# Batch 0 of a fused attention and two-MoE kernel in plain fp32 matmuls, with w_in decoded in another way and a new order of the steps up to batch 1

## The chip, the cores and the metric

The kernel runs on one core of a Trainium2 chip. The metric is the device time of one execution in microseconds, the median of several runs. A core has TensorE (PE; its weight loads are the rows PEld), VectorE (DVE), ScalarE (ACT), GpSimd (POOL) and SyncE (SP), whose queue here issues nearly all DMAs. Each engine takes its instructions in the order in which they were written.

## What is computed

Eight batches of 576 tokens pass an attention with 32 memory slots for each of 8 heads of 64, then a MoE layer with a squared relu (512 to 2048 to 512), then a second one with a softmax-weighted activation and a layer norm (512 to 1024 to 512). The weights are float64.

```python
a = softmax(phi)                    # [8, 8, 576, 32], over axis 2 (the tokens)
k_m = einsum('bhsm,bhsd->bhmd', a, k);  v_m = einsum('bhsm,bhsd->bhmd', a, v)
attn = softmax(q @ k_m.T / 8) @ v_m              # per head: 576 x 32 times 32 x 64
x = attn.transpose(0, 2, 1, 3).reshape(4608, 512)
h = x @ w_in                                     # 4608 x 2048
g = s * relu(h) ** 2 + b
x = g @ w_out                                    # 4608 x 512
# second MoE: h = x @ w_in2; solu = h * softmax(h); (layer norm of solu * g_ln) @ w_out2
```

## The kernel before

For a batch the attention's output is never formed. V·w_in is multiplied first (`vw_mm`, L613: a block matrix of v_m against 512 columns of w_in, four products j = 0 to 3), and the probabilities, transposed, are then multiplied by it: `gemm1_mm` (L982) makes hp, 128 features by 288 tokens, for each half j of the batch and each of 8 pairs of feature blocks. Relu and square (`relu` L993, `square` L1018 or L1020, `square_hi` L1010) make g; `gemm2_mm` (L1043) sums g against w_out into y, for each half j and each of four blocks d of 128 outputs; y goes to DRAM for the second MoE, which follows after batch 7.

fp32 accuracy is had from fp16 matmuls: each operand is split into a high and a low half after a scaling by a power of two (`split_hi` on ScalarE L310, `split_lo` on VectorE L313), and a product is three passes, high by high, high by low and low by high. One hp of two blocks is 12 matmuls of 288 columns, one y 48. The scale needs a bound: for w_in the maximum over all of it, for w_out one over each half. The float64 weights are decoded on the chip from pairs of 32-bit words, in pieces of 128 x 1024: for w_in an absolute value (`decode_abs`, ScalarE, L245), a max pass that also clamps (`decode_max`, VectorE, L255), a shift and a merge of the sign (`decode_bits`, L271 and L262), and the three low bits, either by an OR (`piece_or`, VectorE, L1139) or by a shift and an add on GpSimd (L250 or L252, L268). For w_out it is a scaled copy (`decode_rebias`, ScalarE), a shift and a merge (`decode_shift`, L283, L284) and the OR.

The order up to batch 1 is written out by hand: `FIRST` is a list of steps of which each is one function (`STEPS`), and all engines take their instructions in the order of the list. `Lw.cx` loads piece (c, x) of w_in, `Ai`, `Bi`, `Ci`, `Pi` or `PiX` decode it, `Lo`, `Ao` ... the same for w_out, `km` multiplies k and v by phi, `qm` transposes q, `s0` to `s6` and `sT` are scores and softmax of a third of a batch, `vm` is V·w_in, `g` an hp, `ya` and `yb` the halves of a y, `yo` its eviction, `xh` and `xl` the fp16 halves of w_out, `oad`, `oap`, `oa` the maximum over partitions by a ones-matmul. The digits behind the point are batch or half, then index. `KEEP` gives some steps filler matmuls in front. From batch 1 on a loop runs the same functions, and w_in's and w_out's split halves stay in SBUF. While batch 0 is in work, batch 1's attention is prepared too.

```python
PASSES = ((0, 0), (0, 1), (1, 0))
for step in FIRST.split():
    name, _, at = step.partition(".")
    now[0] = step
    STEPS[name](*(int(a) for a in at))
```

Of the kernel before, what the change touches and what calls it, by code (L numbers as in the profile page):

```python
# [37 lines left out]
s4.01 s1.00 s5P.01 sT.01 phe.1 s0.02 Pi.01 km.10 s1.02 vm.00 s2.00 Lkv.12 ks.10 s3.00 s6P.00 s4.00 s5P.00 im PiX.11
vs0 iad vh.00 s2.02 Pi.30 vm.01 Lkv.13 ko.10 iap vl.00 ia vm.02 km.11 sT.00 vh.01 iv vs.0 Lo.10 ks.11 vl.01 vh.02
vl.02 Ci.31 Lo.01 g.02 Ao.11 Co.11 gr.02 ko.11 PiX.31 gq.02 PoX.11 Ao.10 g.00 gh.02 Lo.00 gr.00 Co.10 Bo.11 gqP.00  # L40
s3.02 g.01 g.05 vm.03 Ao.01 ghD.00 glP.00 gr.01 Co.01 gl.02 g.03 vh.03 gr.05 s6P.02 Lo.21 gqP.01 s4.02 Ao.00 gh.05
PoX.10 mb.1 s5P.02 gqP.05 gh.01 vl.03 Lkv.22 glP.05 Lo.20 gr.03 g.07 Co.00 PoX.01 vb.1 glP.01 gr.07 gqP.03 Bo.00
# [12 lines left out]
yd.10 sT.12 Lq.21
# [10 lines left out]
def tile_mem_attention__moe_relu2__solu_ln(  # L66
# [56 lines left out]
    relu01 = const.tile([128, 1], FP32)  # L123
# [12 lines left out]
    first = gp.tile([128, 1152], FP32, tag="aT", name="first", bufs=2)  # L136
    ones_f = first[:, 256:384]
# [11 lines left out]

    kv_s = kv_p.tile([128, 3, 2, 2, C * D], FP32, name="kv_s")  # L150
# [211 lines left out]
    def load_q(n, i):  # L362
# [1279 lines left out]
```

## Time and profile before

| | |
|---|---|
| median of 3 runs | 1136.35 us (1135.41 to 1138.27) |
| span of the profiled execution | 1132.3 us |
| median less that span | 4.05 us |
| TensorE busy, share of the span | 1074.8 us, 95% |
| VectorE | 793.9 us, 70% |
| ScalarE | 518.6 us, 46% |
| GpSimd | 237.9 us, 21% |
| first matmul of batch 1 | at 189.74 us |

The profile is of one execution. Its rows name a line of the kernel, the engine, the tile written and the tiles read, with sizes and times; an entry in square brackets at a row's end is the time for which the engine had stood idle and the instruction that it waited for. An fp32 matmul has two records. A matmul's record holds its latency too, so a run of records is shorter than the sum of their means. "PEclk" is the granted clock of TensorE: 1.00 is 2.4 GHz, 0.50 is 1.2 GHz. A share of busy time over the whole span mixes stages with different limits, so stretches are read apart.

### The profile page before, as it was taken

To read this page: it belongs to the slowest core of one execution; us is meant where nothing else is said; L and a number is where in the kernel's file an instruction comes from. 1 tells how busy PE (TensorE), PEld (TensorE's weight loads), DVE (VectorE), ACT (ScalarE), POOL (GpSimd) and SP (SyncE) were. 2 spreads that over 40 slices of the span, in tenths; PEclk is the share of its full clock that TensorE was granted. 3 is DMA by queue.
4 is the path that set the end of the run, shared out by engine and by line. 5 is a ranking of instruction groups with operands and counts; after the bars stand their busy time and mean duration, and the time that the engine had idled before them with its cause. 6 is when DMAs were issued, how large, how long until landed. Compare 5 with 4: busy or idle time off the path is not lost.

```text
span 1132.3 us, 20705 instructions
## 1 busy us (share of the span) xinstructions
PE 1074.8 (95%) x8334; PEld 704.9 (62%) x8334; DVE 793.9 (70%) x1516; ACT 518.6 (46%) x753; POOL 237.9 (21%) x182
## 2 busy tenths in 40 slices
PE   4885799998999999999999999999999999999998
PEld 3743567776777777777777777764444444444443
DVE  6899867776876777777677675647666666666662
ACT  2447546455465356365355555623333333333332
POOL 2337341003012012011012020003222222222221
PEclk9688899999999999999999999999999999999999
DMA  9975045594372572643753314114444444445335
GB/s 293 258 204 155 4 107 128 129 216 111 100 178 69 132 156 59 165 124 92 152 143 96 83 25 173 55 52 99 105 100 94 109 106 98 98 112 103 74 76 103
DMA packets 219488, 134.01 MB, mean 118 GB/s; under 512 B 144896, under 2 KB 207616, under 8 KB 219392
## 3 DMA queue, kind: packets, MB, share of 16 engines
q1 hardware_dynamic: 219184, 132.48, 48.0%
q8 instruction: 65, 1.06, 0.4%
q14 instruction: 31, 0.25, 0.1%
q10 hardware_dynamic: 112, 0.20, 0.0%
q0 software_dynamic: 96, 0.01, 0.0%
HBM read 71.83 MB, written 23.07 MB: 84 GB/s over the span
## 4 chain that ended last, share of the span: by engine, by line
PE 75%; DVE 11%; DMA 6%; ACT 3%; issue 2%; SPq 1%; POOL 1%; ACTq 0%; POOLq 0%; DVEq 0%
PE y L1043 26%; PE y L1461 16%; PE hp L1379 16%; PE hp L982 10%; DMA kv_s<-in_k_dram 1%; PE wp L672 1%; DVE g L1025 1%; PE kp L475 1%; DMA work<-in_moe_w_out_dram 1%; PE sp L818 1%; DMA w_in_t<-wt_s 1%; DMA w_out<-in_q_dram 1%; DMA q_s<-in_q_dram 1%; DVE wt_s L313 1%; PE sp L862 1%
## 5 line engine op out<-in xcount | busy, mean ns | idle before, releaser
L1043 PE MATMUL y<-g,w_out 128*128 128x288 f16 (+1 forms) x2880 | 365.5, 287 | 7.5 <-DVE first L197 7.5
L1043 PEld LDWEIGHTS <-w_out 128*128 128x128 f16 x3072 | 297.9, 98 | 101.2 <-issue 21.3
L982 PE MATMUL hp<-aT,vwt 128*128 128x288 f16 x1536 | 197.9, 290 | 19.0 <-ACT r L993 12.6
L1379 PE MATMUL hp<-w_t,xs 128*128 128x512 f16 x864 | 192.0, 379 | 0.0
L1461 PE MATMUL y<-w_t,lt 128*128 128x512 f16 x864 | 191.7, 379 | 0.0
L982 PEld LDWEIGHTS <-vwt 128*128 128x128 f16 x1536 | 152.1, 99 | 62.0 <-issue 15.4
L1461 PEld LDWEIGHTS <-lt 128*128 128x128 f16 x864 | 84.6, 98 | 101.7
L1379 PEld LDWEIGHTS <-xs 128*128 128x128 f16 x864 | 84.5, 98 | 101.4
L1423 POOL TENSOR_TENSOR rstd<-ve,nhalf 128x1 f32<-128x1 f32 x36 | 52.6, 1462 | 333.4 <-DVE mv L1421 333.4
L1393 DVE TENSOR_REDUCE hmx<-hp 128x1 f32<-128x1024 f32 x36 | 44.1, 1224 | 83.9 <-PE hp L1379 83.9
L310 ACT ACTIVATE xs<-xt,xsc 128x512 f16<-128x512 f32 x36 | 25.9, 720 | 150.8 <-PE hp L1379 129.3
L1018 ACT ACTIVATE r<-r 128x576 f32<-128x576 f32 x118 | 80.6, 683 | 21.5 <-DVE g L1025 15.2
L1025 DVE TENSOR_TENSOR g<-r,g 128x576 f16<-128x576 f32 x113 | 87.4, 773 | 3.8
L1060 ACT ACTIVATE x<-y,bcol,cs 128x288 f32<-128x288 f32 x64 | 37.5, 585 | 114.7 <-PE y L1043 102.1
L993 ACT ACTIVATE r<-hp 128x576 f32<-128x576 f32 x120 | 77.1, 642 | 13.6 <-PE hp L982 8.1
L307 DVE TENSOR_REDUCE xmx<-x 128x1 f32<-128x288 f32 x64 | 28.8, 450 | 58.1 <-ACT x L1060 57.2
L967 DVE CAST g<-r 128x576 f16<-128x576 f32 x112 | 51.5, 460 | 20.7 <-ACT r L1018 20.7
L895 POOL TENSOR_TENSOR e<-e,ssm 96x512 f32<-96x512 f32 x22 | 24.8, 1128 | 195.5 <-DVE ssm L890 195.5
L1400 ACT ACTIVATE e<-hp,nm,xiv 128x1024 f32<-128x1024 f32 x36 | 43.3, 1203 | 46.1 <-DVE nm L1395 46.1
L1469 ACT ACTIVATE o<-y,io 128x512 f32<-128x512 f32 x36 | 24.7, 687 | 53.0 <-issue 40.5
L1437 DVE TENSOR_TENSOR nat<-so,nat 128x1024 f16<-128x1024 f32 x36 | 43.7, 1215 | 5.4 <-ACT nat L1432 5.4
L1416 DVE BATCH_NORM_STATS2 bs<-so 128x6 f32<-128x512 f32 x72 | 46.3, 685 | 1.2
(246 smaller groups left out, 1215.6 us busy)
## 6 DMA issues: line engine op xcount, KB each, us to landing
x_d<-x SPq DMA_DIRECT2D x64, 144.0 KB, 2.1
xt<-x_d SPq DMA_DIRECT2D x36, 256.0 KB, 3.2
kv_s<-in_k_dram SPq DMA_DIRECT2D x31, 288.0 KB, 5.9
kv_s<-in_v_dram SPq DMA_DIRECT2D x31, 288.0 KB, 6.5
q_s<-in_q_dram SPq DMA_DIRECT2D x42, 144.0 KB, 3.3
phi_sb<-in_phi_dram SPq DMA_DIRECT2D x8, 576.0 KB, 5.8
out_dram<-o SPq DMA_DIRECT2D x23, 192.0 KB, 2.9
raw<-in_moe_w_out_dram SPq DMA_DIRECT2D x4, 1024.0 KB, 6.8
```

What stands on the lines that cost most here:

```text
L967: nc.vector.tensor_copy(out=g_of(n, j, 0)[:, 2 * fp:2 * fp + 2, 0:BLK], in_=gt["r2", j, fp])
L982: nc.tensor.matmul(out=hp[:, u, 0:BLK], lhsT=vt[:, pw, R, f * 128:(f + 1) * 128], rhs=aT[:, CJ * j:CJ * (j + 1), pa, R, :], start=(x == 0) ...
L993: nc.scalar.activation(out=r, in_=gt.pop(("h", j, fp))[:, :, 0:BLK], func=ACTF.Relu, scale=scale)
L1018: nc.scalar.activation(out=r2, in_=r, func=ACTF.Square)
L1025: (nc.vector if eng == "D" else nc.gpsimd).tensor_tensor(out=g_of(n, j, 1)[:, fs, 0:BLK], in0=gt.pop(("r2", j, fp)), in1=g_of(n, j, 0)[:, ...
L1043: nc.tensor.matmul(out=y[:, 0:w], lhsT=w_out_t[d][:, pw, f, :], rhs=g_of(n, j, pg)[:, f, 0:w], start=(x == 0), stop=(x == len(steps) - 1),)
L1379: nc.tensor.matmul(out=hp[:, a, :], lhsT=xs[:, px, kk, :], rhs=wt[:, pw, kk, a * 512:(a + 1) * 512], start=(kk == 0 and px == 0 and pw == ...
L1393: nc.vector.tensor_reduce(out=mx, in_=hv, op=ALU.max, axis=AX)
L1416: nc.vector.bn_stats(out=bs[:, a, :], in_=so[:, a * 512:(a + 1) * 512])
L1423: nc.gpsimd.tensor_tensor(out=rstd, in0=ve, in1=nhalf, op=ALU.pow)
L1437: nc.vector.tensor_tensor(out=nat[:, 1, :], in0=so, in1=nat[:, 0, :], op=ALU.subtract)
L1461: nc.tensor.matmul(out=y[:, 0:DM], lhsT=lt[:, pl, f, :], rhs=wt[:, pw, f, :], start=(x == 0), stop=(x == len(steps) - 1),)
```

## The change

Batch 0 no longer splits anything. Its hp is an fp32 product of fp32 V·w_in (`first_vw`, a copy out of PSUM) and fp32 transposed probabilities (`first_tr` transposes them on TensorE, `first_aT` copies them); g is fp32 (`first_sq`), and y multiplies it by the decoded fp32 w_out (`first_y`). The fp16 halves of w_out, which later batches use, are still made. The scale of batch 0's V·w_in and relu goes, and the bias column and the factor of y's eviction with it become simpler. w_in is decoded as w_out was: scaled copy, shift and merge, OR on VectorE; its maximum is a plain reduction of the decoded piece at any later time, and GpSimd decodes nothing. The steps s4, s5, sT of batch 0 and its gq, gh, gl go. q of batch 0 is loaded in longer rows, and its transposes are plain matmuls by the identity in two column halves. Some buffers move: w_out's fourth decoded piece lies in a fixed square buffer `r2_s`, k, v and q of batches 0 and 1 lie elsewhere. `KEEP` has 37 filler matmuls where it had 130. `FIRST` is a new list.

```diff
 KEEP = {
-    "km.00": 78, "km.00+": 8, "km.01": 18, "mm.0": 8, "s0.01": 6, "oap.0": 6, "oap.1": 6,
+    "pht.0": 7, "pho.0": 3, "km.01": 1, "mm.0": 11, "qm.00": 4, "qm.02": 6, "at.1": 5,
 }
...
-Lw.21 Lphi.0 Lq.00 Lw.00 LiD.21 Lw.20 Lw.30 Ai.21 qm.00 Bi.21 Ai.20 Lw.01 Ai.30 Ai.00 Lw.10 Ci.21 Ai.10 phm.0 pht.0
+Lphi.0 phm.0 Lw.00 pht.0 Ai.00 Lq.00 Lw.10 Lq.01 phd.0 Lkv.01 pho.0 phb.0 Lkv.00 Ai.10 Lkv.02 phe.0 qm.01 qo.01 qm.00
...
+    def first_tr(cp):
+        ev = sc_e[0, cp].rearrange("p (c h) m -> p c (h m)", c=2)
+        tp = ps_h.tile([128, 2, 512], FP32, tag="h", name="ta")
+        keep(tp[:, 1])
+        for c in range(2):
+            for R in range(2):
+                nc.tensor.transpose(
+                    out=tp[:, 0, (2 * R + c) * P:(2 * R + c + 1) * P], in_=ev[:, c, R * 128:(R + 1) * 128],
+                    identity=ident[0:P, 0:P],
+                )
+        sc_e[0, cp] = tp
...
+    def first_vw(j, R, copy):
...
+        copy(out=vw_t[0][:, R, j * 512:(j + 1) * 512], in_=wp_t[0, j][:, R, :])
...
+    def first_h(j, fp):
+        hp = ps_h.tile([128, 2, 512], FP32, tag="h", name="hp")
...
+            for R in range(2):
+                nc.tensor.matmul(
+                    out=hp[:, u, 0:BLK],
+                    lhsT=vw_t[0][:, R, f * 128:(f + 1) * 128],
+                    rhs=aT0[:, R, CJ * j:CJ * (j + 1), :].rearrange("p c t -> p (c t)"),
+                    start=(R == 0),
+                    stop=(R == 1),
+                )
...
+    def first_sq(j, fp):
+        x = 2 * (fp % 4)
+        nc.scalar.activation(out=g32_of(j, fp // 4)[:, x:x + 2, 0:BLK], in_=gt.pop(("r", j, fp)), func=ACTF.Square)
...
+    def first_y(j, d, part):
...
+        w = BLK + 1 - j
+        wt = wt_t[d, part].rearrange("p (k d) -> p k d", k=8)
+        for f in range(8):
+            nc.tensor.matmul(
+                out=y[:, 0:w], lhsT=wt[:, f, :], rhs=g32_of(j, part)[:, f, 0:w],
+                start=(part == 0 and f == 0), stop=(part == 1 and f == 7),
+            )
...
     def piece_max(c, x):
...
-        decode_max(piece("i", c, x)[0], pk_t["i"][:, 2 * c + x:2 * c + x + 1])
+        src = piece("i", c, x)[0]
+        nc.vector.tensor_reduce(
+            out=pk_t["i"][:, 2 * c + x:2 * c + x + 1], in_=src, op=ALU.max, axis=mybir.AxisListType.XY,
+            apply_absolute_value=True,
+        )
...
-        (decode_abs if w == "i" else decode_rebias)(*piece(w, c, x))
+        decode_rebias(*piece(w, c, x))
...
-        (decode_bits if w == "i" else decode_shift)(*piece(w, c, x))
+        decode_shift(*piece(w, c, x))
```

VectorE's queue at its start, before: a piece of w_in with its max pass (L255), then phi's tree of maxima (L393 to L395).

```order
L252 TENSOR_SCALAR raw<-raw 128x1024
L255 TENSOR_SCALAR w_in_t,pk<-w_in_t 128x2x512
L271 TENSOR_SCALAR w_in_t<-w_in_t 128x2x512
L262 SCALAR_TENSOR_TENSOR w_in_t<-raw,w_in_t 128x2x512
L393 TENSOR_TENSOR t<-phi_sb 96x512
L394 TENSOR_TENSOR t<-t,phi_sb 96x512
L395 TENSOR_TENSOR pm<-t 96x256
L412 TENSOR_REDUCE first<-tx 128x2
L416 TENSOR_TENSOR first<-ident,first 128x256
L444 TENSOR_TENSOR phi_sb<-phi_sb,tx 96x1536
```

The same place now (L383 to L435 is phi, L280, L281 and L1189 a piece of w_in):

```order
L383 TENSOR_TENSOR t<-phi_sb 96x512
L384 TENSOR_TENSOR t<-t,phi_sb 96x512
L385 TENSOR_TENSOR pm<-t 96x256
L402 TENSOR_REDUCE first<-tx 128x2
L406 TENSOR_TENSOR first<-ident,first 128x256
L435 TENSOR_TENSOR phi_sb<-phi_sb,tx 96x1536
L280 TENSOR_SCALAR w_in_t<-w_in_t 128x2x512
L281 SCALAR_TENSOR_TENSOR w_in_t<-raw_g,w_in_t 128x2x512
L1189 SCALAR_TENSOR_TENSOR w_in_t<-raw_g,w_in_t 128x2x512
L280 TENSOR_SCALAR w_in_t<-w_in_t 128x2x512
```

Phi went ahead of all of w_in, and no max pass stands between a piece's shift and the copy before it.

TensorE where batch 0's first y begins, before: the last rows of an hp and the first of y, each matmul with its weight load, w_out in fp16.

```order
L982 LDWEIGHTS vwt
L982 MATMUL hp<-aT,vwt 128x288
L1043 LDWEIGHTS w_out_118
L1043 MATMUL y<-g,w_out_118 128x289
L1043 LDWEIGHTS w_out_118
L1043 MATMUL y<-g,w_out_118 128x289
```

The same place now, from batch 0's last V·w_in (wp) on; hp is L935, k and v by phi L464, y L967, mp (L189) a maximum over partitions:

```order
L603 MATMUL wp<-w_in_t,first 64x512 x4
L935 MATMUL hp<-aT_116,vw_478 128x288 x4
L464 MATMUL kp<-kv_s,phi_sb 32x128 x24
L489 MATMUL kp<-ones,phi_sb 32x1 x24
L935 MATMUL hp<-aT_116,vw_478 128x288 x12
L189 MATMUL mp<-first 128x128
L935 MATMUL hp<-aT_116,vw_478 128x288 x12
L967 MATMUL y<-g_545,wt_s 128x289 x8
L967 MATMUL y<-g_785,wt_s 128x289 x8
L189 MATMUL mp<-first 128x128
L935 MATMUL hp<-aT_116,vw_478 128x288 x4
```

y now reads the decoded w_out (wt_s) in fp32, eight matmuls for a half of the features instead of 24, and the maximum for w_out's scale (the second mp) stands behind the first y instead of ahead of it.

## Rows read from the trace of the kernel before

**Rows 1.** Busy us by stretch (PE, PEld, DVE, ACT, POOL), granted clock, DMA share, GB/s.

```profile
40.00:60.00 20.00, 17.97 (x130) 15.46 (x130) 17.33 (x35) 7.83 (x12) 5.60 (x4) 0.50 0.80 214
70.10:189.70 119.60, 93.88 (x686) 66.20 (x687) 97.18 (x143) 68.54 (x99) 52.24 (x32) 0.90 0.40 105
80.00:100.00 20.00, 11.10 (x59) 7.20 (x59) 17.90 (x22) 12.60 (x20) 14.76 (x9) 0.74 0.84 228
...
120.00:140.00 20.00, 12.54 (x92) 9.38 (x90) 16.52 (x24) 8.34 (x13) 8.03 (x5) 0.83 0.01 1
...
189.70:275.70 86.00, 81.62 (x790) 62.77 (x789) 63.97 (x118) 46.89 (x66) 10.46 (x10) 1.00 0.70 166
275.70:362.00 86.30, 84.89 (x820) 65.45 (x819) 61.99 (x123) 46.06 (x71) 15.09 (x11) 1.00 0.47 120
```

**Rows 2.** TensorE in order of time: start us, us, what, count, idle before.

```profile
41.75 1.19 PE L564 MATMUL tq<-ident,w_out 96*128 96x96 f32 x6 [1.05 <-DMA w_out<-in_q_dram]
...
44.98 2.71 PE L862 MATMUL sp<-kmT,qt_s 128*96 128x64 f32 x16
...
58.86 3.42 PE L613 MATMUL wp<-w_in_t,first 128*64 128x512 f32 x8
...
62.72 1.94 PE L613 MATMUL wp<-w_in_t,first 128*64 128x512 f32 x8
...
67.85 1.52 PE L475 MATMUL kp<-kv_s,phi_sb 96*32 96x128 f32 x48
...
70.12 4.57 PE L982 MATMUL hp<-aT,vwt 128*128 128x288 f16 x36 [0.33 <-DVE vwt L313]
...
91.31 6.38 PE L982 MATMUL hp<-aT,vwt 128*128 128x288 f16 x32 [6.09 <-DVE vwt L313]
...
130.58 4.58 PE L1043 MATMUL y<-g,w_out 128*128 128x289 f16 x24 [7.46 <-DVE first L197]
...
135.65 0.39 PE L192 MATMUL mp<-first 128*128 128x128 f32 x2
...
142.70 12.09 PE L1043 MATMUL y<-g,w_out 128*128 128x289 f16 x96
154.71 3.65 PE L613 MATMUL wp<-w_in_t,work 128*64 128x512 f32 x16
...
189.74 11.92 PE L982 MATMUL hp<-aT,vwt 128*128 128x288 f16 x96
```

**Rows 3.** VectorE in order of time: max, shift, merge, OR; then stretched forms.

```profile
8.07 1.22 DVE L255 TENSOR_SCALAR_CACHE_REDUCE w_in_t<-w_in_t 128x1024 f32<-128x1024 f32 x1 [0.50 <-ACT w_in_t L245]
...
9.33 0.69 DVE L271 TENSOR_SCALAR w_in_t<-w_in_t 128x1024 int32<-128x1024 int32 x1
10.06 1.23 DVE L262 SCALAR_TENSOR_TENSOR w_in_t<-raw,w_in_t 128x1024 int32<-128x1024 int32 x1
...
27.62 1.22 DVE L1139 SCALAR_TENSOR_TENSOR w_in_t<-raw,w_in_t 128x1024 int32<-128x1024 int32 x1
...
86.40 3.28 DVE L1139 SCALAR_TENSOR_TENSOR wt_s<-w_out,wt_s 128x1024 int32<-128x1024 int32 x1
...
104.92 1.27 DVE L313 SCALAR_TENSOR_TENSOR w_out<-wt_s,sc,w_out 128x1024 f16<-128x1024 f32 x1
...
107.77 4.38 DVE L313 SCALAR_TENSOR_TENSOR w_out<-wt_s,sc,w_out 128x1024 f16<-128x1024 f32 x2
```

**Rows 4.** The maxima's ones-matmul, line 192: ns min/median/max, first and last start.

```profile
L192 PEld LDWEIGHTS mp<-first x14: 186/190/337, 47.4 to 135.7; 128*128 128x128 f32 x14
L192 PE MATMUL mp<-first x14: 273/275/527, 47.5 to 135.8; 128*128 128x128 f32 x14
```

**Rows 5.** The page: GB/s in 40 equal slices of the span, 28.3 us each.

```profile
GB/s 293 258 204 155 4 107 128 129 216 111 100 178 69 132 156 59 165 124 92 152 143 96 83 25 173 55 52 99 105 100 94 109 106 98 98 112 103 74 76 103
```

**Rows 6.** The page's costliest groups: busy us, mean ns, idle before; relu on ScalarE.

```profile
L993 ACT ACTIVATE r<-hp 128x576 f32<-128x576 f32 x120 | 77.1, 642 | 13.6 <-PE hp L982 8.1
```

**Rows 7.** The same: a plain max reduction of 1024 columns on VectorE.

```profile
L1393 DVE TENSOR_REDUCE hmx<-hp 128x1 f32<-128x1024 f32 x36 | 44.1, 1224 | 83.9 <-PE hp L1379 83.9
```

More of the change, by code (lines that the diff above doesn't have):

```diff
@@ L38 @@
[L38 to L42, printed above, removed]
@@ L155, in tile_mem_attention__moe_relu2__solu_ln, with keep @@
     now = [""]
-    def keep(out_, key=""):
+    def keep(out_):
         w = min(256, out_.shape[1])
         ones_h = ones_f.bitcast(FP16)
-        for _ in range(KEEP.get(key or now[0], 0)):
+        for _ in range(KEEP.get(now[0], 0)):
             nc.tensor.matmul(out=out_[:, 0:w], lhsT=ones_h[:, 0:128], rhs=ones_h[:, 0:w], start=True, stop=True)
@@ L471, in kv_mm @@
             for i in range(4):
-                if c == 0 and i == 2:
-                    keep(kp[:, 1, 128:512], now[0] + "+")
                 kv = kv_t[n, 2 * g + i // 2]
@@ L562, in q_mm @@
         tp = ps_h.tile([128, 2, 512], FP32, tag="h", name="tq")
+        keep(tp[:, 1, 304:512])
         for c in range(C):
-            nc.tensor.transpose(
-                out=tp[:, c // CJ, (c % CJ) * P:(c % CJ + 1) * P],
-                in_=qt[:, c].rearrange("p h d -> p (h d)"),
-                identity=ident[0:P, 0:P],
-            )
+            for h in range(2):
+                nc.tensor.matmul(
+                    out=tp[D * h:D * (h + 1), c // CJ, (c % CJ) * P:(c % CJ + 1) * P],
+                    lhsT=qt[:, h, c * D:(c + 1) * D],
+                    rhs=ident[0:P, 0:P],
+                    start=True,
+                    stop=True,
+                    tile_position=(0, D * h),
+                )
         tq_t[n, i] = tp
@@ L887, in scores_3 @@
         nc.vector.tensor_scalar(
-            out=sm, in0=sm, scalar1=1e-9, scalar2=2.0 ** -14, op0=ALU.add, op1=ALU.mult
+            out=sm, in0=sm, scalar1=1e-9, scalar2=2.0 ** -14 if n else 1.0, op0=ALU.add, op1=ALU.mult
         )
@@ new lines, in first_vw @@
+    def first_vw(j, R, copy):
+        if 0 not in vw_t:
+            vw_t[0] = gp.tile([128, 2, DFF], FP32, tag="vwt", name="vw0")
+        copy(out=vw_t[0][:, R, j * 512:(j + 1) * 512], in_=wp_t[0, j][:, R, :])
+    def first_h(j, fp):
+        hp = ps_h.tile([128, 2, 512], FP32, tag="h", name="hp")
+        keep(hp[:, 0, 304:512])
+        for u in range(2):
+            f = 2 * fp + u
+            for R in range(2):
[6 more added lines that the diff above has]
+                )
+        gt["h", j, fp] = hp
@@ new lines, in g32_of @@
+    def g32_of(j, a):
+        if (j, a) not in g_t:
+            if j:
+                t = flat((qt_s, q_s)[a]).rearrange("p (f t) -> p f t", f=KF // 2)
+            else:
+                t = gp.tile([128, KF // 2, BLK + 1], FP32, tag=f"g{a}", name="g32")
+                nc.vector.memset(t[:, :, BLK:BLK + 1], 1.0)
+            g_t[j, a] = t
+        return g_t[j, a]
+    def first_sq(j, fp):
+        x = 2 * (fp % 4)
+        nc.scalar.activation(out=g32_of(j, fp // 4)[:, x:x + 2, 0:BLK], in_=gt.pop(("r", j, fp)), func=ACTF.Square)
@@ new lines, in first_y @@
+    def first_y(j, d, part):
+        if part == 0:
+            gt["y", j, d] = ps_y.tile([128, 512], FP32, tag="y", name="y")
+        y = gt["y", j, d]
+        if part == 0:
+            keep(y[:, 304:512])
+        w = BLK + 1 - j
+        wt = wt_t[d, part].rearrange("p (k d) -> p k d", k=8)
+        for f in range(8):
+            nc.tensor.matmul(
+                out=y[:, 0:w], lhsT=wt[:, f, :], rhs=g32_of(j, part)[:, f, 0:w],
+                start=(part == 0 and f == 0), stop=(part == 1 and f == 7),
+            )
@@ L1015, in square @@
         r = gt["r", j, fp]
-        r2 = rp.tile([128, 2, BLK], FP32, tag="r2", name="r2")
+        used["r2"] = used.get("r2", 1) ^ 1
+        r2 = r2_s[:, used["r2"]]
         if eng == "A":
@@ L1036, in gemm2_mm @@
         y = gt["y", j, d]
-        keep(y[:, 304:512])
-        w = BLK + 1 if n == 0 and j == 0 else BLK
+        w = BLK
         steps = [(f, pw, pg) for f in range(KF) for pw, pg in PASSES]
```

136 lines of the change are left out of this document (51 added, 85 removed).

## The prediction

> **What bounds the kernel now.** I read three views. The busy time by stretches comes first [rows 1]: from 189.7 us on, when batch 1's first matmul starts, TensorE is busy 81.6 of 86.0 us in batch 1 and 84.9 of 86.3 us in batch 2. Its own work is the bound there, and the change leaves the code of batches 1 to 7 as it is. Before 189.7 us TensorE is the bound only at the very end: it works 11.1 of 20 us from 80 to 100 and 12.5 of 20 from 120 to 140, while VectorE is at 17.9 and 16.5. So the question is one number: when does the first matmul of batch 1 start, 189.74 us now?
>
> The second view is TensorE in order of time [rows 2]. Batch 0's first scores run at 44.98, its first product of the MoE (hp) at 70.12. Between lie the decoding of w_in and the scale of the fp16 split: from 40 to 60 the granted clock is 0.50, the lower of its two levels (1.2 GHz) [rows 1]; 16 records of scores take 2.71 us there, the first product V·w_in 3.42, and the next one, once the clock is back, 1.94. Behind 70.12 come gaps: 6.09 us for VectorE's low half of a split (vwt), 7.46 us for a maximum of w_out that waits behind w_out's decoding. From 142.7 on TensorE is nearly full.
>
> The third view is VectorE [rows 3]. A piece of w_in costs it a max pass (1.22), a shift (0.69), a merge (1.23) and an OR (1.22) of 1024 columns; a low half costs 1.27. While GpSimd works, the same forms stretch: the OR to 3.28, two low halves to 4.38 where 2.5 is their own price.
>
> **TensorE's side of the change.** It removes 192 + 384 fp16 matmuls of 288 columns (16 pairs of blocks x 12, 8 outputs x 48) and puts 64 + 128 fp32 ones in their place. The price of an fp16 one is 12.09 us for 96, so 0.126, and 576 make 72.5 us [rows 2]. The price of an fp32 one: 8 records of the V·w_in product take 1.94 us and 16 take 3.65, so 8 more cost 1.71; two records make one matmul and two column halves run at once, so 512 columns take 0.428 us for one record, or 0.835 ns a column. A record of 288 columns is 0.24 us, a matmul 0.48; with some 5 ns of start for each record, 0.49, and 192 make 94 us. From above: 1.94 / 4 = 0.485 us for 512 columns gives 0.273 a record and 105 us. I take 94, from the longer run of records, which a stream of 128 resembles most. So TensorE gets 21.5 us more work. It pays only because that work needs no scale, no split and no second copy of an operand.
>
> A weight of these matmuls is a full 128x128 fp32 tile, loaded anew for each record: 384 loads. The one full tile in the trace, a maximum's ones-matmul, multiplies its two records of 128 columns in 0.39 us [rows 2]; a single record takes 0.273 and a single load 0.19 [rows 4], so the second starts 0.117 after the first, against 0.107 for 128 columns at 0.835 ns. The load lies beneath the stream, and I price it at nothing.
>
> The Trainium skill speaks against this: "TensorE: Matmul & The Clock Gate", Part 3 (Packing small matmuls), has a load overlap a running matmul only when they use different rows of the array, and all rows are used here. By that rule each record would wait for its load, and the sum would be the third rival below; the 0.117 us just read does not agree with it, though it is one pair of records.
>
> **The front, up to batch 0's first hp.** The new order puts phi first and issues only phi (0.59 MB), four w_in pieces (4 x 1.05), four k/v pairs (4 x 0.59) and eight q halves (8 x 0.147) ahead of the last q that the scores need: 8.3 MB. The first slice of the page, 28.3 us, moved 293 GB/s [rows 5], which is 8.3 MB; before, two more w_in pieces and q in short pieces lay in that stretch. So q is there at 28.5. Then in a chain: two q transposes (1.19 each at half clock) and a copy (0.64 for 576 columns), to 31.5 [rows 2, 6]; two scores at half clock 2 x 2.71, to 37; the first V·w_in 3.42, to 40.4; five filler matmuls and the transposes of the probabilities, now on TensorE instead of by DMA, about 2; the second V·w_in 1.9 to 3.4; transposes and the third score another 2. First hp at 46 to 49; I take 47, against 70.12. VectorE stays ahead of it: w_in's four first pieces at 0.69 + 1.23 + 1.22 = 3.1 us with no max in front, the last landing near 26, so done by 33. The max (a plain reduction now, 1.22 us by the nearest row [rows 7]) moves behind, since only batch 1 needs it. The filler matmuls go from 130 to 37; they ran where TensorE had nothing else (78 of them in front of the first k/v product). Their removal costs clock at most, and I priced this part at half clock for that reason.
>
> **From the first hp to batch 1.** TensorE's work there, in order: 94 for the fp32 products; two V·w_in of batch 0 and four of batch 1, 6 x 1.83 = 11; two k/v products of batch 1 with their sums, 2 x 2.1 = 4.2 (1.52 for the product); three scores of batch 1, 2.6; maxima and small transposes, 4. Sum 116. Before, the same stretch took 189.74 - 70.12 = 119.6 us, of which 93.9 were TensorE's [rows 1]. VectorE in this stretch, piece by piece from [rows 3, 7]: four w_in pieces and six max passes 20, w_out's eight pieces 25, its eight low halves 10, batch 1's four low halves 5, q 8, softmax 14 and 3, phi 9, scales and maxima some 11: 105 us of the 116. ScalarE is well below (16 x 2 passes over hp at 0.64 [rows 6], 20 us, and some 60 us of splits and decoding). GpSimd has nearly nothing left to do there, so VectorE's forms should keep their short price. VectorE also takes the softmax product from GpSimd, 3 x 0.7, counted.
>
> What is late next: where w_out's low halves were on the path (they had to be there before a y could start), y now reads the decoded fp32 itself, and the halves are needed only by batch 1. The queues, held against each other, wait in three places. ScalarE decodes the first w_out pieces in the middle of batch 0's relus; where such a load lands late, the relus behind it hold hp's three buffers, and TensorE stands. With the pieces in order that is 1 to 2 us in all; phi's ones-matmul before the second max of phi holds VectorE's next w_in piece and so V·w_in, 1 us; and the last softmax of batch 1 and its DMA transpose end within 1 us of TensorE's last y. I add 4.
>
> The sum: 47 + 116 + 4 = 167, against 189.7: 22.7 us earlier. Batches 1 to 7 follow at their own pace. The profiled span of 1132.3 becomes 1109.6; the median lies 4.05 above the span, so 1113.6, and I say 1113.
>
> **Rivals.** *VectorE becomes the bound.* 105 us of work in 116 leave little slack, and its queue is in order. For it: in the old stretch VectorE was busy 97.2 of 119.6 us, 81% [rows 1]. At that share 105 us take 130, batch 1 starts at 177, and the time is 1124. Against it: the old 81% had waits for GpSimd and for scales in it that are gone. 0.20.
>
> *TensorE without waits, earlier start.* If the clock is full from 30 us on and w_in's pieces arrive at the rate of the start, first hp is at 44; with 92.4 for the products the rest is 114: batch 1 at 158, time 1104. For it: between the first and the second V·w_in product, 58.86 and 62.72, the clock came back though the first is fp32 alone [rows 2]. 0.14.
>
> *The fp32 weights are not hidden (slower).* If each of the 384 records waits for the whole of its load, 0.19 us [rows 4], that is 73 us more: batch 1 at 240, 50 us later than now, time 1186. It decides from 23 / 384 = 0.06 us a record, a third of a load. For it: no stream of full fp32 tiles is in the trace. Against it: the 0.117 us above, and the fp16 stream, where each 0.126 us holds a load too. 0.06.
>
> That the earlier start is given back in batch 1 would need its inputs to come late; batch 1 has 4.4 us of idle TensorE, and its k, v, q loads are issued behind the same steps as before, so I give no case of its own to it; it is in the range.
>
> **Numbers.** Forecast (1107 to 1119): 0.60; VectorE bound 0.20; earlier still 0.14; slower 0.06. The measurement can tell 0.3%, 3.4 us. A sixth of the VectorE case reaches back to no change or beyond, so faster 0.89, same 0.03, slower 0.08. The range takes in 1104 from below and the VectorE case with 5 us on top: 1102 to 1129.
>
> **What would show it.** First hp at 46 to 49 and not later; records of the new products 0.24 to 0.25 us apart; VectorE's ORs at 1.22 throughout; batch 1's first matmul at 164 to 170. Wrong: records over 0.30 apart (third rival); TensorE's idle time ahead of y put down to VectorE's decoding of w_out, or ahead of hp to ScalarE's relu (first rival); half clock after 50 us, which would double the price of what runs there; batch 1 taking more than 88 us.

## The result, and the profile after the change

| | before | after, first set | after, once more |
|---|---|---|---|
| median, us | 1135.94 (4 runs) | 1118.08 (1114.06 to 1120.45, 4 runs) | 1115.66 (1113.11 to 1118.52, 5 runs) |
| ratio to before on the same chip | | 0.9835 (0.9812 to 0.9858) | 0.9819 (0.9795 to 0.9844) |
| span of the profiled execution | 1132.3 | 1118.7 | 1113.9 |
| first hp of batch 0 at | 70.12 | 53.98 | 46.96 |
| first hp to batch 1's first matmul | 119.62 | 121.01 | 123.41 |
| batch 1's first matmul at | 189.74 | 174.99 | 170.37 |

The forecast was 1113 with a range of 1102 to 1129. The change is faster by 18 to 20 us (1.7 to 1.8%), clear of the spread of both kernels; some 23 were expected (1136.35 to 1113). Two profiles stand in the table because the two profiled executions of the same kernel differ in the front, which the argument needs.

The page of the first profile: TensorE is busy 97% of the span where it was 95%, GpSimd 15% where it was 21%. The first slice moved 245 GB/s, where [rows 5] had 293.

```profile
PE 1090.3 (97%) x8129; PEld 717.3 (64%) x8129; DVE 771.2 (69%) x1486; ACT 509.9 (46%) x746; POOL 171.3 (15%) x143
...
GB/s 245 291 233 158 33 112 108 165 183 77 166 125 92 158 119 92 163 120 79 182 95 96 78 39 193 40 43 109 99 110 100 92 113 104 90 109 104 77 75 104
```

TensorE in order of time, first profile; it answers to [rows 2]. L555 transposes q, L852 and L808 are the scores of batch 0 and 1, L603 is V·w_in, L935 hp, L967 y, L1036 batch 1's hp.

```profile
35.43 0.58 PE L555 MATMUL tq<-ident,q_s 96*64 96x96 f32 x2 [0.97 <-DMA q_s<-in_q_dram]
...
40.20 5.38 PE L852 MATMUL sp<-kmT,qt_s 128*96 128x64 f32 x32
45.51 3.68 PE L603 MATMUL wp<-w_in_t,first 128*64 128x512 f32 x8
50.26 1.94 PE L603 MATMUL wp<-w_in_t,first 128*64 128x512 f32 x8
...
53.98 4.15 PE L935 MATMUL hp<-aT,vw 128*128 128x288 f32 x16
...
149.54 0.27 PE L808 MATMUL sp<-work 128*96 128x64 f16 x2 [0.66 <-DMA work<-kv_s]
152.61 3.56 PE L808 MATMUL sp<-work 128*96 128x64 f16 x42 [2.79 <-DMA work<-kv_s]
...
171.11 4.04 PE L967 MATMUL y<-q_s,r_s 128*128 128x288 f32 x16
174.99 11.92 PE L1036 MATMUL hp<-aT,vwt 128*128 128x288 f16 x96
```

Between 53.98 and 174.99 there are only the two bracketed waits: the gaps of 6.09 and 7.46 us of the kernel before are gone. The stretches of the same profile (columns as in [rows 1]) show the rest: TensorE is full from 54 to 145, at 152, behind the wait, the clock is at 0.50, and batch 1 takes 90.07 us where it took 86.0, batch 2's first matmul coming at 265.06.

```profile
54.00:145.00 91.00, 91.00 (x559) 66.16 (x559) 76.27 (x128) 54.69 (x81) 4.82 (x3) 1.00 0.50 144
145.00:152.00 7.00, 4.16 (x22) 3.05 (x20) 6.62 (x12) 7.00 (x7) 0.00 (x0) 0.99 0.76 95
152.00:158.00 6.00, 5.39 (x46) 4.87 (x47) 3.89 (x7) 3.67 (x6) 0.00 (x0) 0.50 1.02 285
...
174.99:265.06 90.07, 84.17 (x790) 63.70 (x789) 64.52 (x118) 47.38 (x67) 11.85 (x9) 0.96 0.70 157
```

The second profile of the same kernel has another front. The scores run at 3.22 us for 32 records and the first V·w_in at 1.94, and the first hp comes 7 us earlier; behind it stand the wait for the transposed q, which both profiles have, and a new one of 2.40 us for the exp of batch 1's phi.

```profile
33.31 2.00 PE L555 MATMUL tq<-ident,q_s 96*64 96x96 f32 x24
35.08 1.22 PE L555 MATMUL tq<-ident,wt_s 96*64 96x96 f32 x24
36.23 3.22 PE L852 MATMUL sp<-kmT,qt_s 128*96 128x64 f32 x32
39.38 1.94 PE L603 MATMUL wp<-w_in_t,first 128*64 128x512 f32 x8
...
46.96 4.15 PE L935 MATMUL hp<-aT,vw 128*128 128x288 f32 x16
...
64.12 1.60 PE L464 MATMUL kp<-kv_s,phi_sb 96*32 96x128 f32 x47 [2.40 <-ACT phi_sb L441]
149.12 2.21 PE L808 MATMUL sp<-work 128*96 128x64 f16 x42 [2.87 <-DMA work<-kv_s]
```

### The profile page after: what moved, and what is told of

It is laid out like the page before. It is cut to its first block, busy times and chain, and to the rows that moved or that the text cites. A ratio compares the mean times of both kernels' runs of the same rounds, so it can differ in the third digit from the quotient of the medians.

```text
span 1118.7 us, 20178 instructions
## 1 busy us (share of the span) xinstructions
PE 1090.3 (97%) x8129; PEld 717.3 (64%) x8129; DVE 771.2 (69%) x1486; ACT 509.9 (46%) x746; POOL 171.3 (15%) x143
## 3 DMA queue, kind: packets, MB, share of 16 engines
q8 instruction: 64, 1.05, 0.4%
## 4 chain that ended last, share of the span: by engine, by line
PE 83%; DMA 6%; DVE 6%; ACT 2%; SPq 1%; issue 1%; POOL 0%; ACTq 0%; POOLq 0%; DVEq 0%
PE y L1091 24%; PE y L1497 17%; PE hp L1415 17%; PE hp L1036 11%; PE y L967 4%; PE hp L935 3%; DMA q_s<-in_q_dram 2%; PE wp L662 2%; PE kp L464 2%; PE sp L808 1%; DMA w_in_t<-wt_s 1%; DVE g L1074 1%; PE wp L603 1%; DMA kv_s<-in_v_dram 1%; DMA work<-in_moe_w_out_dram 1%; DVE wt_s L310 1%
## 5 line engine op out<-in xcount | busy, mean ns | idle before, releaser
L1091 PE MATMUL y<-g,w_out 128*128 128x288 f16 x2688 | 340.5, 287 | 0.0
L1091 PEld LDWEIGHTS <-w_out 128*128 128x128 f16 x2688 | 260.5, 98 | 80.6 <-issue 10.6
L1036 PE MATMUL hp<-aT,vwt 128*128 128x288 f16 x1344 | 167.4, 286 | 2.5 <-ACT r L1047 2.5
L1036 PEld LDWEIGHTS <-vwt 128*128 128x128 f16 x1344 | 131.5, 98 | 36.3 <-issue 3.1
L1047 ACT ACTIVATE r<-hp 128x576 f32<-128x576 f32 x128 | 82.3, 643 | 18.6 <-PE hp L935 8.1
L1074 DVE TENSOR_TENSOR g<-r_s,g 128x576 f16<-128x576 f32 x112 | 85.6, 765 | 3.9
L1067 ACT ACTIVATE r_s<-r 128x576 f32<-128x576 f32 x112 | 76.6, 684 | 18.4 <-DVE g L1074 15.0
L1108 ACT ACTIVATE x<-y,bcol,cs 128x288 f32<-128x288 f32 x56 | 32.8, 585 | 102.3 <-PE y L1091 95.5
L1021 DVE CAST g<-r_s 128x576 f16<-128x576 f32 x112 | 51.4, 459 | 19.7 <-ACT r_s L1067 19.7
L1447 DVE SCALAR_TENSOR_TENSOR so<-hp,sm,e 128x1024 f32<-128x1024 f32 x36 | 46.2, 1284 | 1.3
```

The costliest lines, as they stand in the source:

```text
L1021: nc.vector.tensor_copy(out=g_of(n, j, 0)[:, 2 * fp:2 * fp + 2, 0:BLK], in_=gt["r2", j, fp])
L1036: nc.tensor.matmul(out=hp[:, u, 0:BLK], lhsT=vt[:, pw, R, f * 128:(f + 1) * 128], rhs=aT[:, CJ * j:CJ * (j + 1), pa, R, :], start=(x == 0) ...
L1047: nc.scalar.activation(out=r, in_=gt.pop(("h", j, fp))[:, :, 0:BLK], func=ACTF.Relu, scale=scale)
L1067: nc.scalar.activation(out=r2, in_=r, func=ACTF.Square)
L1074: (nc.vector if eng == "D" else nc.gpsimd).tensor_tensor(out=g_of(n, j, 1)[:, fs, 0:BLK], in0=gt.pop(("r2", j, fp)), in1=g_of(n, j, 0)[:, ...
L1091: nc.tensor.matmul(out=y[:, 0:w], lhsT=w_out_t[d][:, pw, f, :], rhs=g_of(n, j, pg)[:, f, 0:w], start=(x == 0), stop=(x == len(steps) - 1),)
```

## The experiments

All are edits of the changed kernel but e8, which is one of the kernel before. Edits of the order are shown as the words of `FIRST` that move. "hp" is the first hp, "b1" batch 1's first matmul.

| run | hp | hp to b1 | b1 | median, us |
|---|---|---|---|---|
| e1, more fillers | 50.00 | 122.21 | 172.21 | 1114.04 |
| e2, q first | 47.63 | 120.17 | 167.80 | 1112.36 |
| e3, scores later | 47.67 | 122.86 | 170.53 | 1114.04 |
| e4, a quarter of y left out | 47.21 | 112.90 | 160.11 | 1105.17 |
| e5, again | 46.96 | 123.41 | 170.37 | 1115.66 |
| e6, exp first | 54.23 | 121.04 | 175.27 | 1116.08 |
| e7, e2 + e3 + e6 | 48.27 | 116.81 | 165.08 | 1108.72 |
| e9, narrow y | 48.94 | 114.48 | 163.42 | 1108.68 (one run) |
| e10, e7 with the old q | 51.28 | 116.82 | 168.10 | 1112.20 |
| e11, e7 without e3 | 47.70 | 122.81 | 170.51 | 1114.93 |
| e12, e7 and a copy earlier | 48.33 | 116.13 | 164.46 | 1109.56 |

### e1: more filler matmuls in the front

```diff
-    "pht.0": 7, "pho.0": 3, "km.01": 1, "mm.0": 11, "qm.00": 4, "qm.02": 6, "at.1": 5,
+    "pht.0": 7, "pho.0": 3, "qm.01": 28, "km.01": 8, "mm.0": 11, "qm.00": 4, "qm.02": 11, "at.1": 5,
```

> More filler matmuls where TensorE waits in the front: 28 ahead of the first q transposes (it waited 5.9 us for q there), 8 instead of 1 ahead of the second k/v product, 11 instead of 6 ahead of the third q. Theory 1 (TensorE runs the front at half pace because it works too little early: scores 5.38 us for 32 records against 3.0 at the pace of the third score, first V.w_in 3.68 against 1.94, k/v 2.79 against 1.52): with the waits filled the first hp comes at 48 to 50 instead of 54, batch 1's first matmul as much earlier, time -4 to -6 us. Rival (q, landing at 35 to 36, and the last piece of w_in, decoded at 39.1, set the front): the same records run faster but first hp moves by less than 2 us.

TensorE's stretches, columns as in [rows 1]:

```profile
20.00:24.00 4.00, 4.00 (x64) 3.78 (x66) 2.40 (x3) 0.64 (x1) 0.00 (x0) 0.50 1.11 236
28.00:32.00 4.00, 3.54 (x90) 2.97 (x83) 0.13 (x1) 1.15 (x1) 0.00 (x0) 0.50 1.05 298
32.00:36.00 4.00, 4.00 (x22) 3.22 (x21) 3.59 (x6) 1.19 (x5) 0.00 (x0) 0.50 1.08 227
36.00:40.00 4.00, 3.78 (x58) 2.98 (x56) 2.92 (x3) 2.25 (x3) 0.00 (x0) 0.93 1.02 372
```

The first hp at 50 lies in theory 1's interval, but not for its reason: the clock stood at 0.50 from 16 to 36 although TensorE worked nearly without a gap, and rose as late as 37. Unfilled, e5's front was 3 us earlier. In this execution the fillers did not bring the clock earlier; that they never do, one profile of a front that differs between executions (e5) can't show. The median is within the spread of the unedited kernel.

### e2: q ahead of two pieces of w_in

```diff
-... Ci.10 Bi.00 Lw.11 km.00 ... mv.0 Lq.02 qm.02 Lq.03 Ai.01 ...
+... Ci.10 Bi.00 Lq.02 Lq.03 Lw.11 km.00 ... mv.0 qm.02 Ai.01 ...
```

> The loads of the last two pairs of q heads stand ahead of the third and fourth piece of w_in on SyncE's queue. Theory 2 (the step that failed is q's arrival: its loads were issued at 20.4 to 24.5, behind two 1 MB pieces): q lands at 29 to 31, scores start at 35 to 36 instead of 40.2, first hp at 49 to 51, time -3 to -5 us. Rival (w_in's pieces, now later by the 0.59 MB of q, some 2.4 us, are the next limit, or TensorE's half pace): first hp at 52 or later, time within 2 us.

TensorE no longer waits for this q: its transposes start at 32.99, right behind the fillers, and run at 1.21 us for 24 records. The scores come at 35 to 39, hp at 47.63. That is earlier than theory 2 had it, since the front ran at full pace, and no earlier than e5 had it with q in the old place. What TensorE waits for there now is a copy of the transposed q (0.73 us at 36) and the softmax of the probabilities (1.54 us at 43). The runs, 1111.73 to 1115.79, overlap with those of the unedited kernel.

### e3: batch 1's scores one y part later

```diff
-... y.031 vl.11 s0.10 s0.11 Lkv.22 ... y.120 s3.10 ...
+... y.031 vl.11 Lkv.22 ... y.120 ym.03 s0.10 s0.11 ... s3.10 ...
```

> Batch 1's scores stand one y part (16 records, 4.0 us) later. Theory 3 (TensorE's two waits of 0.66 and 2.79 us for the transposed q, and the half clock from 152 to 158.6 behind them, cost 5 to 6 us): waits below 1 us, granted clock 1.00 throughout, batch 1's first matmul at 169 to 170 instead of 175.0, time -5. Rival (the softmax and its transposes then end last): TensorE waits for the transposed probabilities ahead of batch 1's first hp, and the time moves by less than 2 us.

The waits for the transposed q are gone (the 48 scores run in 2.31 us), and b1 comes at 170.53 with 0.60 us of waiting for the transposed probabilities. But the gain was taken by a wait at the front, and ScalarE in order of time shows its cause:

```profile
61.79 1.14 ACT L276 ACTIVATE w_in_t<-w_out 128x1024 f32<-128x1024 f32 x1 [4.12 <-DMA w_out<-in_moe_w_in_dram]
...
64.09 1.47 ACT L441 ACTIVATE phi_sb<-phi_sb 96x1536 f32<-96x1536 f32 x1
```

A piece of w_in lands late, ScalarE stands in front of its decoding for 4.12 us, and the exp of batch 1's phi (L441), ready since 58.9 on VectorE's side, is queued three instructions behind, with a relu and a square between. TensorE waits for it 3.17 us at 62.4, and the 16 records of hp that follow take 7.08 us instead of 4.15:

```profile
69.02 7.08 PE L935 MATMUL hp<-aT,vw 128*128 128x288 f32 x16
```

In the first profile, with hp 6 us later, nothing waits there.

### e4: a quarter of y left out

```diff
-        for f in range(8):
+        for f in range(6):
...
-                start=(part == 0 and f == 0), stop=(part == 1 and f == 7),
+                start=(part == 0 and f == 0), stop=(part == 1 and f == 5),
```

> Batch 0's y takes 12 of its 16 feature blocks only, so a quarter of the sum is left out: 32 fp32 matmuls fewer. Theory (TensorE is the bound from the first hp on, a matmul 0.487 us): batch 1's first matmul 15.6 us earlier, at 159 to 160, time -15 us. Rival (VectorE, with 105 us of work in that stretch, or the DMA of the transposed q stands right behind TensorE): batch 1's first matmul at 167 or later, time -8 us or less, and the difference appears as TensorE's waits.

TensorE lost 15.6 us of work, and hp to b1 shrank by 10.5 against e5 and 8.1 against the first profile. b1 at 160.11 meets the theory's 159 to 160 by luck: those were counted from a first hp at 54, and it came at 47.21. TensorE's longest waits from 47 to 161 (us in total, times, longest):

```profile
PE mp L189 <- DVE first L183: 4.4, 1, 4.4
PE kp L464 <- ACT phi_sb L441: 2.2, 1, 2.2
PE sp L808 <- DMA work<-kv_s: 1.4, 2, 1.2
PE hp L1036 <- DMA aT<-a: 1.2, 1, 1.2
PE wp L603 <- ACT work L540: 1.1, 1, 1.1
```

TensorE is the bound of the stretch, but not by far: the largest wait is for VectorE, ahead of the maximum of w_out's second half. Of 15.6 us less work 8 to 10.5 were gained, and of 27 us less no more (e9).

### e5: the changed kernel once more

> The changed kernel as it is, once more. In its first profile the front ran at half pace until 48 us and the first hp came at 54.0; in two of the experiments whose front is the same instructions, the pace rose at 24 and again at 34 and the first hp came at 47.2 and 47.7. Theory 4 (the granted clock in the front differs from execution to execution, and the 7 us by which the forecast missed the first hp are that): runs spread over 5 us or more, the fastest near 1113, and if the profiled one is among the faster, its first hp comes at 47 to 48. Rival (the first profile is the rule, the experiments moved the front): all runs within 3 us around 1118, first hp at 53 to 54 again.

Theory 4 holds for the profiled execution, with hp at 46.96, and the runs reach from 1113.11 to 1118.52. That the front is what sets the other runs apart is not shown, since only one of them has a profile; nor is what decides between the two fronts. In the executions with hp at 54 (the first profile and e6) q landed at 35.4 to 35.6, after TensorE had stood for it 1.1 to 2.4 us; in e5, e3, e4 and e9 it was there at 34 or earlier. But e3 and e9 waited 0.9 and 1.1 us for it too, and their pace came back all the same. That stays open.

### e6: the exp ahead of the late piece

```diff
-... Lo.11 g.01 ... aA.2 Lw.31 ... gs.02 Ai.31 gr.13 Ci.31 gs.13 ... Ci.30 phe.1 km.10 ...
+... Lw.31 Lo.11 g.01 ... aA.2 ... gs.02 phe.1 gr.13 gs.13 Ai.31 Ci.31 ... Ci.30 km.10 ...
```

> The exp of batch 1's phi stands ahead of the decoding of w_in's seventh loaded piece on ScalarE, and the load of the eighth ahead of the first two of w_out. Theory 5 (with the first hp at 47, TensorE waits 3.2 us for that exp, since ScalarE stands 4.1 us for the piece's load in front of it): that wait is below 0.5 us; first hp to batch 1's first matmul 118 to 120 us (116 of work and the waits for the transposed q) instead of 121 to 123; time -3 against e5 where the fronts are alike. Rival (the piece itself is next: its V.w_in then waits as long): the wait moves to another instruction within 10 us, first hp to batch 1 at 121 or more.

Its profiled execution had the late front (hp at 54.23), in which the exp is not waited for anyway, so of that wait it settles nothing. It has a new one, of 1.38 us at 73 for a copy of V·w_in, which e7, e10 and e11 have too; e12 looks into it. The run's times reach from 1112.65 to 1120.7.

### e7: e2, e3 and e6 together

> The q loads ahead of two w_in pieces, batch 1's scores one y part later, the exp ahead of the decoding, together. If the three waits add up: first hp at 47, batch 1's first matmul at 164 to 165 (116 to 117 us of TensorE work between), time 1107 to 1109. Rival (the softmax of batch 1 and its transposes end last, 0.6 us late already with the scores later): TensorE waits for the transposed probabilities by 2 us or more, batch 1 at 167 or later, time 1111 or more.

```profile
48.27 4.15 PE L935 MATMUL hp<-aT,vw 128*128 128x288 f32 x16
...
68.44 2.21 PE L935 MATMUL hp<-aT,vw 128*128 128x288 f32 x8 [1.39 <-ACT vw L927]
165.08 11.92 PE L1036 MATMUL hp<-aT,vwt 128*128 128x288 f16 x96 [0.60 <-DMA aT<-a]
```

These are all of TensorE's waits from hp on. 116.81 less 1.99 leaves 114.8 us of work. The forecast of b1 and of the time came out, with hp 1.3 us later than expected: 1108.72 (1108.33 to 1109.96), a ratio of 0.9759 (0.9738 to 0.9781) to the kernel before, and its runs lie within 1.6 us, where the two sets of the unedited kernel lie within 6.4 and 5.4. It is the fastest kernel of this study that leaves nothing out, some 7 us below the change. The three edits don't add up singly: against the change's 1115.66, e3 alone has 1114.04 and the other two without it 1114.93 (e11), since the wait that is left costs the clock behind it each time.

### e11: e7 with the scores back in their place

> As e7, but batch 1's scores stand where the change has them. Theory (TensorE's wait for the transposed q and the clock behind it are paid on the path): waits of 3 to 3.5 us ahead of the scores, first hp to batch 1's first matmul 120 to 121 instead of 116.8, time +3 to +4, 1112 to 1113. Rival (they are made good by the next wait for the softmax): within 1 us of e7.

```profile
144.86 0.28 PE L808 MATMUL sp<-work 128*96 128x64 f16 x2 [0.59 <-DMA work<-kv_s]
147.70 3.22 PE L808 MATMUL sp<-work 128*96 128x64 f16 x42 [2.56 <-DMA work<-kv_s]
150.73 6.24 PE L967 MATMUL y<-qt_s,wt_s 128*128 128x288 f32 x16
```

```profile
148.00:154.00 6.00, 6.00 (x47) 5.14 (x45) 4.85 (x8) 4.06 (x6) 0.00 (x0) 0.52 0.88 251
```

The wait costs twice: 3.15 us of standing, and then 16 records of y take 6.24 us instead of 4.04 and the 42 scores 3.22 instead of 2.08 (e1), with the clock at 0.52 from 148 to 154. 6.0 us in all (122.81 against 116.81), and 6.2 in the median; the expectation had counted the first part alone. The Trainium skill describes this in "TensorE: Matmul & The Clock Gate", section "HAM oscillation — how this bites in real kernels": waits for DMA between groups of matmuls bring the clock down, and the next group starts slow. The rows agree.

### e10: e7 with q loaded and transposed as before

```diff
-            nc.sync.dma_start(out=t[:, a], in_=q[n, 2 * i + a].rearrange("(p c) d -> p (c d)", c=C))
+                nc.sync.dma_start(out=t[:, :, a, :], in_=q[n, 2 * i + a].rearrange("(p c) d -> p c d", c=C))
```

> As e7, but with q of batch 0 loaded and transposed as before the change: rows of 256 bytes and 6 transposes of 128 columns for a pair of heads instead of rows of 1.5 KB and 24 records of 64. Theory (the longer rows pay): q lands 1 to 3 us later, the transposes take 1.2 instead of 2.2 us at half pace, first hp 48 to 50 and time 0 to +3 against 1108.7. Rival (the transposes in 24 records are the dearer part): first hp at 47 or earlier, time -1 or less.

The short rows make everything land later: TensorE waits 1.44 us at 37 for the copy of the transposed q, half pace follows, hp comes at 51.28. The longer rows with their 24 records for 6 are worth 3 us of hp here, which is less than two executions of one kernel can differ by (e5), but also 3.5 in the median, and the runs (1111.16 to 1113.31) lie above all of e7's: a little more than the theory had.

### e12: V·w_in's copy earlier on VectorE

```diff
-... Lo.10 Ci.30 km.10 ks.10 vD.21 ...
+... Lo.10 vD.21 Ci.30 km.10 ks.10 ...
```

> As e7, with the copy of V.w_in's third product ahead of two pieces of w_in on VectorE. In e7 TensorE waited 1.39 us for that copy at 68 us. If VectorE's order is the cause, the wait goes and batch 1's first matmul comes at 163.5 to 164, time -1.4 against e7, 1107.3. Rival (w_in's pieces, now 0.7 us later, hold the fourth V.w_in): within 0.5 us of e7.

The wait of 1.39 us goes, and half of it comes back at the next product:

```profile
69.78 2.12 PE L603 MATMUL wp<-w_in_t,first 128*64 128x512 f32 x8 [0.73 <-DVE w_in_t L1189]
```

b1 at 164.46 is 0.6 earlier; the medians, 1109.56 and 1108.72, don't tell the two kernels apart.

### e9: half of y's columns

```diff
-                out=y[:, 0:w], lhsT=wt[:, f, :], rhs=g32_of(j, part)[:, f, 0:w],
+                out=y[:, 0:u], lhsT=wt[:, f, :], rhs=g32_of(j, part)[:, f, 0:u],
```

Here `u` is 144, but `w` in the first and the last matmul of each sum.

> The changed kernel, but batch 0's y is summed over 144 of its 288 columns except in the first and last matmul of each sum, so half of it is left out: 112 of the 128 matmuls have 144 columns and the same full fp32 weight tiles. It measures when the weight loads come out from under the stream. Theory (they are hidden, the stream sets the price, 0.835 ns a column): records 0.12 us apart, 0.25 us a matmul. Rival (a load takes some 0.19 us, as a single one does, and is hidden only because a record of 288 columns takes 0.243): records 0.17 us or more apart.

```profile
106.66 2.37 PE L968 MATMUL y<-g,r_s 128*128 128x144 f32 x16
108.87 2.36 PE L968 MATMUL y<-qt_s,wt_s 128*128 128x288 f32 x16
111.06 2.36 PE L968 MATMUL y<-q_s,r_s 128*128 128x144 f32 x16
```

From one start to the next it is 2.19 to 2.21 us for 16 records, of which two are wide (0.243 each); the other 14 take 0.122 each. Even at half the columns the load of a full fp32 tile, 0.19 us when nothing covers it, adds nothing. Removing 27 us of TensorE work (224 records by 0.121) shortened hp to b1 by 8.9 against e5 and 6.5 against the first profile. The rest goes into waits, as in e4: 4.0 us for VectorE ahead of maxima and 3.8 for the transposed q are the largest.

### e8: the kernel before, its w_in decoded without GpSimd

```diff
-... LiD.21 ... LiA.30 ... LiD.01 ... LiA.00 ... LiA.10 ... Pi.21 ... Pi.10 ... Pi.00 ... Pi.01 ... Pi.30 ...
+... PiX.21 ... PiX.10 ... PiX.00 ... PiX.01 ... PiX.30 ...
```

> The kernel before, with all of w_in's low bits joined by an OR on VectorE (1.22 us each), none by a shift and an add on GpSimd: one part of the change alone. Theory (GpSimd's share of the decoding is not what held the kernel before; its max pass, scales and low halves were): VectorE has some 5 us more in the front, the stretched OR goes from 3.28 to 1.22, first hp 69 to 72, batch 1's first matmul 188 to 192, time within 3 us. Rival (the change's gain is GpSimd gone from w_in's decoding): first hp 62 to 66, time -4 us or more.

```profile
75.02 4.57 PE L982 MATMUL hp<-aT,vwt 128*128 128x288 f16 x36 [0.33 <-DVE vwt L313]
...
91.31 3.27 DVE L1139 SCALAR_TENSOR_TENSOR wt_s<-w_out,wt_s 128x1024 int32<-128x1024 int32 x1
```

The seven ORs of w_in up to 75 us took 1.21 to 1.22 each, and hp comes 4.9 us later than in [rows 2], about what VectorE got to do in addition (five ORs more, two shifts of 0.69 fewer). b1 comes at 194.15, and the median is 1137.75 against 1135.81. That part of the change gains nothing by itself. The expected hp of 69 to 72 was too early; the 4.9 us fit a front that VectorE held and not GpSimd. The expected end of the stretched OR did not come either: it is one of w_out's, and takes 3.27 where it took 3.28 [rows 3], so GpSimd's decoding of w_in was not what stretched it.

## Why the prediction was right, and where it was not

**The price of the fp32 products held.** From start to start, 16 records of y take 171.11 to 174.99, 3.88 us, 0.243 a record and 0.485 a matmul; priced at 0.49 (the 5 ns of start that the price added to a record come out at 2, 0.2425 less 0.2405). The loads are hidden, as priced (nothing), down to 144 columns. The third rival falls, and with it the rule of the Trainium skill that was weighed against the trace ("TensorE: Matmul & The Clock Gate", Part 3): these loads use all rows of the array and overlap all the same.

**TensorE's work in the stretch held.** 116 predicted; 114.8 in e7 and e12, once their waits are taken off.

**The waits were the wrong ones.** 4 us were added for three places. Of these only the last, the transposed probabilities, is seen, with 0.6 us in e3 and e7. What stood there instead, in e5: 2.40 for the exp of phi and 2.87 for the transposed q, and 3.3 us lost to half clock behind them (123.41 less 5.27 less 114.8). The mechanism of the first was in the text (ScalarE stands at a late load and what is queued behind it waits), but the load was w_in's seventh piece and not w_out's. The second was not: batch 1's q comes out of its split by DMA transposes, and its scores stood in TensorE's order ahead of y parts that could run meanwhile (e3). A wait was priced at its length, without the clock behind it; in the first profile that is 2.8 us (121.01 less 3.45 less 114.8), with the half clock from 152 to 158 that the text named as a sign of error. So the stretch met its 120 in part by luck: 6.2 and 8.6 us stood where 4 were added, with 1.2 less work beside them, and b1 came at 174.99 and 170.37, behind the 164 to 170 that were named.

**First hp at 47 was hit once, by two errors that cancel.** The step that failed is q's landing: 28.5 predicted, 33 to 35.5 measured. SyncE's queue in the first profile shows why:

```profile
18.04 0.38 SPq L1128 DMA_DIRECT2D raw<-in_moe_w_in_dram  x1
19.25 0.38 SPq L1128 DMA_DIRECT2D raw_g<-in_moe_w_in_dram  x1
20.44 1.53 SPq L360 DMA_DIRECT2D q_s<-in_q_dram  x2
22.82 1.65 SPq L360 DMA_DIRECT2D wt_s<-in_q_dram  x2
```

The last q pairs are issued at 20 to 24, each of their four loads only when an earlier load of k or v has landed (3.4 us of SyncE's waits), and take 14.7 and 13.4 us (medians of two) to land, sharing the way with 1 MB pieces issued just ahead. And the rate was 249 GB/s from 8 to 20, while k, v and q came in, not 293; that mean was of another mix of loads. Over the first 34 us it is 252:

```profile
0.00:34.00 34.00, 20.70 (x277) 16.02 (x278) 17.14 (x29) 7.84 (x10) 2.96 (x9) 1.00 0.97 252
```

At that rate the text's 8.3 MB take 33 us: most of the error is the rate. From q's landing the chain to hp was priced at 18.5 us, at half pace, and in the first profile it took 18.5 (35.43 to 53.98), so that 47 + 7 = 54. In its parts that is luck too: q's transposes and copies took 4.8 us instead of 3.0 (24 records for a pair of heads, where rows of 6 had been priced), and from the end of the first V·w_in to hp it was 4.8 instead of 6.6, since the pace had come back (the second V·w_in took 1.94). In e5 the chain ran at full pace from 35 on, and the 5 us that q was late came back. Up to 50 us the choice of pace was a choice, and the runs show both.

**VectorE was not the bound, but near.** 0.20 was given to it. Its work came out near the 105 us of the text: 101.05 from 54 to 175 in the first profile. In the changed kernel TensorE never waits for VectorE between hp and b1; with a quarter of y gone it does at once (e4).

**Batch 1 gave some back, though its code is the same.** More than 88 us there was named as a sign of error, and it took 90.1 and, in e5, 90.3. TensorE in the first profile:

```profile
220.53 4.57 PE L1036 MATMUL hp<-aT,vwt 128*128 128x288 f16 x36 [1.96 <-ACT r L1047]
...
248.29 1.90 PE L662 MATMUL wp<-w_in_t,work 128*32 128x512 f16 x16 [3.56 <-DVE e L825]
250.12 8.09 PE L1091 MATMUL y<-g,w_out 128*128 128x288 f16 x48
```

The kernel before has both waits too, 0.75 and 3.25 us long, but behind the second its V·w_in took 1.05 and its y 6.09: the clock did not fall there.

```profile
261.54 1.05 PE L672 MATMUL wp<-w_in_t,work 128*32 128x512 f16 x16 [3.25 <-DVE e L835]
262.52 6.09 PE L1043 MATMUL y<-g,w_out 128*128 128x288 f16 x48
```

Of the 4.1 us that batch 1 is longer, 1.2 us are the first wait, 2.9 the clock behind the second. In e7, where that wait is 2.32, the clock stays and batch 1 takes 87.5. From batch 2 on 3 us come back (of 2.4 us of waits for relus before, 0.2 are left), so that from b1 to the end it was 942.6 us before and 943.7 and 943.5 after: to give it no case of its own was right by the sum, and not by its reason.

**The offset was mis-sized.** A run's time is its span and 1.8 us (1120.45 and 1118.7, 1115.66 and 1113.9). The 4.05 of the text was the distance of a median to the span of an execution that was itself some 2 us below it. For e5 the sum reads: 0 for hp, +3.4 for the stretch, +0.9 for the rest, -2.3 for the offset, +2.0 in all, 1113.6 to 1115.7. For the first profile +7.0, +1.0, +1.1 and -2.3, to 1120.4.

## What to carry to other kernels

Plain fp32 matmuls can beat a split in three fp16 passes for a stage whose engines wait for scales and halves: here TensorE got 21.5 us more work, which filled the 25.7 us of gaps between hp and b1 (119.60 less 93.88 [rows 1]), and hp itself came 16 to 23 us earlier. The products in fp32, the decoding of w_in and the new order came in one change, and only the decoding without GpSimd was run alone (e8): how much of the 16 to 23 us is the arithmetic's and how much the order's is not shown. The next waits here were for loads that a queue stood at in order, with something urgent behind them; look for such places on every queue. The clock can fall behind a wait of some 3 us and cost about as much again (e3, e11), though in the kernel before it did not fall behind 3.25. When executions of one kernel differ, take two profiles before explaining the first.

## What the runs showed of the hardware

- The granted clock in a row can be 1.00 while the engine runs at half pace. From 36 to 48 the first profile's row says 1.00, and 32 score records take 5.38 us there, as long as at a granted 0.50 [rows 1, 2] (two groups of 16 at 2.71). At full pace they take 3.22 (e5). The duration of a known record tells the pace; the column only does once it has changed in that trace.

```profile
36.00:48.00 12.00, 11.84 (x85) 9.78 (x86) 6.70 (x10) 3.85 (x6) 0.00 (x0) 1.00 1.07 261
```

- A full 128x128 fp32 weight tile is loaded beneath a stream of as little as 144 columns: 0.122 us a record (e9).
- VectorE's stretched form is rare without GpSimd, not gone: one merge of 1024 columns took 4.47 us beside GpSimd's subtraction of phi, where the others took 1.23. The two start within 0.04 us, and the merge ends 1.08 us behind the subtraction, as if it had waited for it.

```profile
128.86 3.43 POOL L435 TENSOR_TENSOR phi_sb<-phi_sb,px 96x1536 f32<-96x1536 f32 x1 [7.58 <-issue]
128.90 4.47 DVE L281 SCALAR_TENSOR_TENSOR r_s<-raw,r_s 128x1024 int32<-128x1024 int32 x1
```
